# Attention pipeline: where the routing units, the table operations and the experts' first transposes stand in the order of work

## The chip, the cores and the metric

The kernel runs on one core of a Trainium2 chip. The metric is the device time of one execution in microseconds (us). The engines are TensorE (PE for its matrix products, PEld for its weight loads), VectorE (DVE), ScalarE (ACT), GpSimd (POOL) and SyncE (SP, which issues transfers). Each takes its own instructions strictly in the order in which they are written and waits for the others by semaphores.

## The reference

Sliding window attention with sinks, then a mixture of experts over its output, all in float32:

```python
B, H, S, D = 4, 8, 768, 64;  n_sink, window = 4, 128
scores = scale * np.matmul(q, k.transpose(0, 1, 3, 2))
scores = np.where(is_sink | in_window, scores, -1e9)
a = np.exp(scores - scores.max(-1, keepdims=True))
a = a / (a.sum(-1, keepdims=True) + 1e-09)
x = np.matmul(a, v).transpose(0, 2, 1, 3).reshape(3072, 512)      # the tokens

g_idx = np.argmax(x @ w_group, axis=1)              # 4 groups
e_idx = np.argmax(x @ w_expert[g], axis=1)          # 4 experts in each, within the token's group
out[token] = softmax(group)[g_idx] * softmax(expert)[e_idx] * (np.maximum(x @ w1[g, e], 0) @ w2[g, e])   # F = 1024
```

## The kernel before, in words

**Attention.** The 3072 tokens are 24 tiles of 128 rows (`NI`), six to a sequence (`NT`). A loop `for i in range(NI + 2)` runs as a pipeline over them: step i makes the scores of tile i, transposes the weights of tile i-1 and multiplies them with the values, and finishes tile i-2 ("old", `b`). The heads come in two groups of four. On VectorE one step is: a predicated copy that puts the sinks in (`ps<-selu,ps`), four masked maxima (`sm<-ps,msk`), the same again for the second group, in even steps the reduction and reciprocal of the sums (`rc`), the normalised logits (`lw`), the row normalisation `norm(b)` (`xt<-po,rc`, which writes the finished rows), and what stands behind it. ScalarE makes the exponentials (`pt`), copies the transposed weights (`pw`, once for each group) and the values (`xT`). GpSimd masks the copied weights with a triangle (`pw<-pw,tri`, once for each group). TensorE's products of step i+1 with the values (`po<-pw,vv`) come behind the `xt` of step i, since both use `po`; `xt` itself comes behind the sinks' product (`po<-spT,sv`).

**Routing.** A generator, `route_batch`, does the routing of six tiles at a time, in small VectorE instructions ("units"), and yields between them. There are four batches; three of them ("early") run within the attention loop, the fourth in its tail. A yield tells of what kind the next piece is: `None` is a plain unit, "pe" stands ahead of products on TensorE, "rd" ahead of a VectorE instruction that reads them, and "hv" ahead of a table operation. The loop takes pieces at fixed places by `routing(k, kinds)`, which takes up to k pieces if the next one is of a kind that is wanted. `unit(k)` takes one plain unit; a step has a quota of eight (`REND`). Units stand between the maxima of the second group (two places), ahead of `norm` (four) and at the end of the step (two); "rd" and "hv" pieces stand only behind `norm`. The names in the profile: `rev`, `m` (shown as `ps`), `rdt`, `req`, `og`, `oh` open a batch (one-hots of group and expert), `pe`, `rs`, `runb`, `pos`, `ge`, `ga` count the position of each token in its expert, `row`, `rm`, `rss` make its gate; a table operation is `bf` on VectorE (one-hot of the position) with `af` on GpSimd, two halves to a batch; the product `tp<-af,bf` is then added to `tab`. From the table come the indices of an expert's tokens (`sel`, `gidx`, `idz`, `sidx`), and from the counts the choice of the next expert (`cnt`, `ktmp`, `cs`, `key`, `ktop`, `keid`, `eid`).

A part of the small tiles of batches 0 and 1 (`keep`) lives in PSUM, in the bank of the second group's scores (`psb[1]`, shown as `ps`); those of batch 2 live in SBUF.

**Weights.** Each expert weight is split in two parts, `whi` on ScalarE and `wlo<-rw,whi` on VectorE. From step 18 on a step may hold such a split of 128x512; its VectorE half (`late()`) stands behind `norm`.

**The tail and the experts.** After the last tile the loop runs two more steps (i = 24, 25) in which the experts begin: `early_work` transposes the first expert's two token tiles (`ph<-ident,xg`; `xpose`, which also casts them on ScalarE and takes the rest on VectorE, both named `un`), then starts its first layer (`ph<-un,whi`). After the loop the experts run one after the other.

All instructions carry line 105, that of the helper that issues them, so groups are told apart by names.

Of the kernel before, what the change touches and what calls it, by code (L numbers as in the profile page):

```python
# [24 lines left out]
NT = S // P  # L25
NI = B * NT
# [29 lines left out]
XLEAD = 9  # L56
PEGAP = 1.6
REND, TSTEP = 8, 16
UNITS = {}
HC = 3  # L60
LATE = 6
PELAG = 2.0
# [72 lines left out]
def moe_attention(tc, kqT, vN, vS, nsw, wgx, w1, w2, out):  # L135
    nc = Pinned(tc)
    v = nc.vector
    with ExitStack() as top, ExitStack() as att:
# [38 lines left out]
        psb = [ps_s.tile([P, 4, 256], F32, name=f"ps{g}") for g in range(2)]  # L177
        PART = 3 * BW + NSK + MAXB
# [174 lines left out]
        def put_gates(n):  # L353
            for _ in range(min(n, len(gates))):
                t, g = gates.pop(0)
                nc.sync.dma_start(xd[t * P:(t + 1) * P, DM:XW], g)
# [7 lines left out]
        def route_batch(i0, nb, lt, wk, pt, tab, na, pick=None):  # L364
# [3 lines left out]
            early = pt is None and not tail  # L368
# [7 lines left out]
            keep = early and pick in (None, 0)  # L376
# [18 lines left out]
            o5 = sm([nk, 4], "req")  # L395
# [4 lines left out]
            yield  # L400
            v.tensor_reduce(m, o5a, AX.X, ALU.max)
            yield
            og = psb[1][:, :, PART - nb:PART].rearrange("p c n -> p n c") if keep else o5[:, :, 0]
            if keep:
                o5b, mb = (t.rearrange("p a (b k) c -> p a b k c", k=nk) for t in (o5a, wide(m)))
                v.tensor_tensor(og.rearrange("p (a b) c -> p a b c", a=na2), o5b[:, :, :, 0], mb[:, :, :, 0], ALU.is_equal)
            v.tensor_tensor(o5a, o5a, wide(m), ALU.is_equal)
# [1 line left out]
            oh = wk.tile([P, nb, NE], BF16, name=f"oh{nb}", bufs=1)  # L409
            v.tensor_tensor(oh.rearrange("p n (g e) -> p n g e", g=G), o5[:, :, 1:],  # L410
                            og[:, :, :, None].to_broadcast([P, nb, G, EG]), ALU.mult)
            yield "pe"
            pp = misc(pt)
            pc = pp[:, nb * NE:(nb + 1) * NE]
# [277 lines left out]
        regs, raws, wt, half, held = {}, [], {}, [], {}  # L692
# [213 lines left out]
        rb = []  # L906
# [308 lines left out]
        def early_work(q):  # L1215
            plan.update(todo=[], at=0, next=0)
            for j in range(q["nt"]):
                xpose(q, j, True)
                yield 0.43
            for k, us in enumerate(layer1_wide(q)):  # L1220
                if k == LATE:
                    wait_for("late")
                    xpose(PARTS[0][1], 0, True)
                yield us

        quota = [0]

        def unit(k):
            if quota[0] > 0 and routing(1, (None,)):
                quota[0] -= 1  # L1230

        ew = early_work(PARTS[0][0])
        load_s(0)
        for i in range(NI + 2):
            live = i < NI
            quota[0] = UNITS.get(i, REND)
            a, b = i - 1, i - 2
            mid, old = 0 <= a < NI, 0 <= b < NI
            state["clk"] += 3.0
            if i == NI:  # L1240
                flush()
                state.update(gap=0.0, dve=state["clk"])
                sps.close()
                put_gates(MAXB)
                while later:
                    gather(*later.pop(0))
                ps_h = fl.enter_context(tc.tile_pool(name="ps_h", bufs=4, space=PSUM, side="right", reuse_waits="tile"))
                tail.append(ps_h)
            if live:
                scores(i, 0)  # L1250
            if mid:
                evac(a, 0)
            if i == NI and half:
                half.pop()()()
            if old:
                if b < NI - 1:
                    values(b, 1)
                out_evac(b)
            if live:
                load_v(i)  # L1260
                scores(i, 1)
                issue()
                maxima(i, 0)
                warm(FILL[i] if i < len(FILL) else 0, tp2[:, 0, 256:448])
            if mid:
                sink_copy(a)
                halves(a, 0)
            if i == NI + 1:
                state["at"] = 0.0
                routing(1, ("pe",))  # L1270
            if mid:
                if not live:
                    next(ew)
                    next(ew)
                sink_t(a)
                trans(a, 1)
            if live:
                exps(i, 0, (0, 1))
            if mid:
                evac(a, 1)  # L1280
                sink_evac(a)
            if live:
                exps(i, 0, (2, 3))
            if mid and not live:
                halves(a, 1)
            if not live and later and not gates:
                gather(*later.pop(0))
            late = None
            if live:
                late = half.pop()() if half else wjob()  # L1290
                if half and i % NT == 0:
                    first, more = late, half.pop()
                    late = lambda: (first(), more()())
            if i == 0:
                late_consts()
            if i == 1:
                routing_consts()
            if live:
                maxima(i, 1, lambda k: unit(k) if k else None)
            if old:  # L1300
                natural(b)
            state["clk"] += 3.0
            if old:
                logits(b)
            if live and mid:
                values(a, 0)
            if i % 2 == 0 and 0 < i <= NI:
                sums(i - 1)
            if not live:
                norm(b)  # L1310
                norm_logits(b)
                next(ew)
            if mid and not live:
                values(a, 0)
            add_heads()
            routing(1, ("pe",))
            if mid:
                sink_values(a)
            if live and old:
                norm_logits(b)  # L1320
            if live:
                if mid:
                    halves(a, 1)
                flush()
                exps(i, 1)
                trans(i, 0)
                for k in range(4):
                    unit(k)
                if old:
                    norm(b)  # L1330
                if later and not gates:
                    gather(*later.pop(0))
                put_gates(2)
                if late:
                    late()
                routing(1, ("rd",))
                routing(1, ("hv",))
                for k in range(2):
                    unit(k)
            else:  # L1340
                if mid:
                    values(a, 1)
                    next(ew)
                put_gates(MAXB)
                routing(TSTEP, (None, "rd", "hv"))
            if old:
                del env[b]
            if i >= CHOOK:
                prefetch(min(RAW, len(raws) + (1 if live else RAW)))
            if not live:  # L1350
                wjob()
                next(ew, None)
# [295 lines left out]
```

## Time and profile before

| what | value |
|---|---|
| median of 3 runs | 487.56 us (487.55 to 487.65) |
| the profiled execution | 487.55 us, its span 485.7 us, 1.85 us around it |
| granted clock of TensorE, mean | 0.998 |
| busy, share of the span | PE 95%, DVE 70%, ACT 67%, POOL 34% |
| attention with routing | up to about 150 us of the span, then the experts |

A busy share over the whole span mixes two stages: the attention loop, in which four engines hand work to each other within a step of some 5 to 7 us, and the experts, in which TensorE alone has hardly a gap. In the timeline's rows a bracket behind a row is the idle time of that engine ahead of it, and what ended it.

### The profile page before, as it was taken

To read this page: it belongs to the slowest core of one execution; us is meant where nothing else is said; L and a number is where in the kernel's file an instruction comes from. 1 tells how busy PE (TensorE), PEld (TensorE's weight loads), DVE (VectorE), ACT (ScalarE), POOL (GpSimd) and SP (SyncE) were. 2 spreads that over 40 slices of the span, in tenths; PEclk is the share of its full clock that TensorE was granted. 3 is DMA by queue.
4 is the path that set the end of the run, shared out by engine and by line. 5 is a ranking of instruction groups with operands and counts; after the bars stand their busy time and mean duration, and the time that the engine had idled before them with its cause. 6 is when DMAs were issued, how large, how long until landed. Compare 5 with 4: busy or idle time off the path is not lost.

```text
span 485.7 us, 15514 instructions
## 1 busy us (share of the span) xinstructions
PE 462.8 (95%) x5865; PEld 394.7 (81%) x5865; DVE 341.5 (70%) x1143; ACT 325.9 (67%) x875; POOL 163.8 (34%) x269
## 2 busy tenths in 40 slices
PE   7999999998879999999999999999999999999994
PEld 6887778776768987989888778797979788877894
DVE  6766787888897799893075256563788888788870
ACT  4898889889884353772265275655778787687961
POOL 3463675565656022323203033012402160205021
PEclk9999999999999999999999999999999999999999
DMA  6566567577764469795124388858969997968200
GB/s 192 162 200 206 192 181 215 181 232 259 263 203 137 132 202 360 242 360 217 47 70 148 109 282 289 306 218 305 381 216 373 410 384 249 301 210 298 63 26 31
DMA packets 49556, 107.47 MB, mean 221 GB/s; under 512 B 8932, under 2 KB 9444, under 8 KB 49472
## 3 DMA queue, kind: packets, MB, share of 16 engines
q1 hardware_dynamic: 45008, 93.17, 56.7%
q0 software_dynamic: 4320, 12.94, 7.7%
q8 instruction: 48, 0.79, 0.7%
q10 hardware_dynamic: 144, 0.28, 0.2%
q14 instruction: 36, 0.29, 0.2%
HBM read 93.58 MB, written 12.93 MB: 219 GB/s over the span
## 4 chain that ended last, share of the span: by engine, by line
PE 65%; DVE 13%; issue 8%; ACT 6%; DMA 4%; POOL 2%; SPq 1%; POOLq 0%; DVEq 0%; ACTq 0%
PE po L105 29%; PE ph L105 28%; PE tp L105 4%; PE ps L105 4%; DVE wlo L105 3%; ACT pt L105 2%; DVE sm L105 2%; DVE xt L105 2%; ACT whi L105 1%; DMA rw<-in_w 1%; DVE un L105 1%; DMA vv<-in_vN 1%; DVE ps L105 1%; DMA ni<-in_nsw 1%; SPq L105 1%
## 5 line engine op out<-in xcount | busy, mean ns | idle before, releaser
L105 DVE TENSOR_TENSOR wlo<-rw,whi 128x1024 fp32r<-128x1024 f32 (+1 forms) x116 | 134.9, 1187 | 28.3 <-ACT whi L105 27.9
L105 PE MATMUL ph<-un,whi 128*128 128x256 f32 (+9 forms) x576 | 128.8, 313 | 0.1
L105 PE MATMUL po<-whi,un 128*128 128x512 f32 (+6 forms) x384 | 126.3, 394 | 0.0
L105 ACT CAST whi<-rw 128x1024 fp32r<-128x1024 f32 (+1 forms) x116 | 114.8, 1018 | 5.7 <-PE po L105 3.5
L105 POOL DMA_INDIRECT out<-ot,sidx x33 | 41.7, 1264 | 221.0 <-ACT ot L105 164.3
L105 PE MATMUL ph<-un,wlo 128*128 128x160 f32 (+10 forms) x416 | 99.6, 265 | 0.2 <-DVE wlo L105 0.2
L105 PEld LDWEIGHTS ph<-un,whi 128*128 128x128 f32 x576 | 94.0, 189 | 2.4 <-issue 0.6
L105 PEld LDWEIGHTS po<-whi,un 128*128 128x128 f32 (+5 forms) x384 | 69.8, 183 | 19.3 <-issue 2.1
L105 ACT ACTIVATE pt<-sm,st 128x136 f32<-128x136 f32 x192 | 76.2, 404 | 7.9 <-DVE st L105 7.7
L105 PE MATMUL po<-wlo,un 128*128 128x512 f32 (+7 forms) x200 | 77.9, 389 | 0.0
L105 PEld LDWEIGHTS ph<-un,wlo 128*128 128x128 f32 x416 | 76.8, 190 | 0.8 <-DVE wlo L105 0.4
L105 POOL TENSOR_TENSOR pw<-pw,tri 128x512 f32<-128x512 f32 x40 | 51.6, 1289 | 17.9 <-ACT pw L105 17.0
L105 DVE CUSTOM_DVE_ANT_0 sm<-ps,msk 128x136 f32<-128x136 f32 x192 | 46.3, 296 | 7.2 <-ACT xT L105 1.4
L105 PE MATMUL po<-pw,vv 64*64 64x128 f32 (+1 forms) x1408 | 40.9, 250 | 7.0 <-POOL sp L105 2.3
L105 PEld LDWEIGHTS po<-pw,vv 64*64 64x64 f32 x1408 | 34.9, 133 | 13.4 <-POOL sp L105 8.2
L105 POOL DMA_INDIRECT xg<-xd,gidx x33 | 35.1, 1065 | 29.4 <-DMA rw<-in_w 16.1
L105 PE MATMUL ps<-kb,qb 64*64 64x204 f32 (+1 forms) x768 | 41.9, 331 | 3.1 <-DVE bf L105 2.1
L105 PEld LDWEIGHTS po<-wlo,un 128*128 128x128 f32 (+6 forms) x200 | 35.7, 179 | 7.8
L105 DVE TENSOR_TENSOR hc<-ph,hc 128x160 f32<-128x160 f32 (+6 forms) x64 | 21.5, 337 | 26.2 <-ACT hc L105 26.2
L105 ACT ACTIVATE un<-ph 128x256 fp32r<-128x256 f32 (+1 forms) x40 | 15.3, 383 | 36.4 <-PE ph L105 36.0
L105 ACT ACTIVATION_READ_ACCUMULATOR pt<-sm,st 128x1 f32 x192 | 37.2, 194 | 0.0
L105 ACT ACTIVATE ot<-po,cg 128x512 f32<-128x512 f32 (+7 forms) x25 | 17.0, 679 | 29.3 <-PE po L105 29.2
(226 smaller groups left out, 654.6 us busy)
## 6 DMA issues: line engine op xcount, KB each, us to landing
rw<-in_w SPq DMA_DIRECT2D x128, 512.0 KB, 5.9
kb<-in_kqT SPq DMA_DIRECT2D x23, 272.0 KB, 4.6
qb<-in_kqT SPq DMA_DIRECT2D x24, 256.0 KB, 3.7
vv<-in_vN SPq DMA_DIRECT2D x24, 256.0 KB, 3.7
xd<-xt SPq DMA_DIRECT2D x24, 256.0 KB, 2.7
xg<-xd,gidx POOLq DMA_INDIRECT x33, 5.8
out<-ot,sidx POOLq DMA_INDIRECT x33, 5.9
sv<-in_vS SPq DMA_DIRECT2D x4, 128.0 KB, 3.7
```

The costliest lines, as they stand in the source:

```text
L105: r = f(*a, **k)
```

## The change

1. Ahead of `norm`, `fill(n)` takes the place of up to four `unit`s: n is 2 in even steps (those with the sums), 4 in odd steps, and 0 where the tile that is normalised is the first of a sequence (i = 2, 8, 14, 20). `fill` takes plain units and table operations ("hv"), and a table operation counts as two.
2. Behind `norm` the order was `late()`, "rd", "hv", two units. It is now "rd", `fill` of two (five where there was none ahead of `norm`; one less in a step with a weight split), and then `late()`.
3. `og` of batch 2 goes to PSUM too while `oh` is made, with one small instruction more; later uses read it in SBUF as before.
4. In step 24 the transposes of the first expert's two token tiles stand ahead of the split and of the products with the values, no longer behind them.

```diff
-UNITS = {}
+HOLE = 2, 4
@@ route_batch
-            og = psb[1][:, :, PART - nb:PART].rearrange("p c n -> p n c") if keep else o5[:, :, 0]
-            if keep:
+            og = psb[1][:, :, PART - nb:PART].rearrange("p c n -> p n c") if early else o5[:, :, 0]
+            if early:
...
             oh = wk.tile([P, nb, NE], BF16, name=f"oh{nb}", bufs=1)
             v.tensor_tensor(oh.rearrange("p n (g e) -> p n g e", g=G), o5[:, :, 1:],
                             og[:, :, :, None].to_broadcast([P, nb, G, EG]), ALU.mult)
+            og = og if keep else o5[:, :, 0]
             yield "pe"
@@ the loop
+        def fill(n):
+            while n > 0 and quota[0] > 0:
+                big = bool(rb) and rb[0][2] == "hv"
+                if not routing(1, (None, "hv")):
+                    return
+                n -= 1 + big
+                quota[0] -= 1 + big
...
-            quota[0] = UNITS.get(i, REND)
+            quota[0] = REND
...
-            if i == NI and half:
-                half.pop()()()
+            if i == NI:
+                next(ew)
+                next(ew)
+                if half:
+                    half.pop()()()
             if old:
                 if b < NI - 1:
                     values(b, 1)
...
             if mid:
-                if not live:
-                    next(ew)
-                    next(ew)
                 sink_t(a)
                 trans(a, 1)
...
-                for k in range(4):
-                    unit(k)
+                fill(HOLE[i % 2] if i % NT != 2 else 0)
                 if old:
                     norm(b)
                 if later and not gates:
                     gather(*later.pop(0))
                 put_gates(2)
+                routing(1, ("rd",))
+                fill((2 if i % NT != 2 else 5) - (late is not None))
                 if late:
                     late()
-                routing(1, ("rd",))
-                routing(1, ("hv",))
-                for k in range(2):
-                    unit(k)
```

VectorE around the row normalisations of steps 18, 19 and 20, the maxima left out. Before:

```order
L105 TENSOR_TENSOR xt<-po,rc 128x2x4x64
L105 TENSOR_TENSOR wlo<-rw,whi 128x512 x2
L105 TENSOR_TENSOR bf<-colm,ps_99 128x384
L105 COPY_PREDICATED ps_98<-selu,ps_98 128x4x64
...
L105 TENSOR_TENSOR xt<-po,rc 128x2x4x64
L105 TENSOR_TENSOR wlo<-rw,whi 128x512
L105 TENSOR_TENSOR bf<-colm,ps_99 128x384
L105 COPY_PREDICATED ps_98<-selu,ps_98 128x4x64
...
L105 TENSOR_TENSOR xt<-po,rc 128x2x4x64
L105 TENSOR_TENSOR wlo<-rw,whi 128x512
L105 TENSOR_TENSOR tab<-tab,tp 128x112
```

The same place with the change, up to the split of step 19:

```order
L105 TENSOR_TENSOR bf<-colm,ps_99 128x384
L105 TENSOR_TENSOR xt<-po,rc 128x2x4x64
L105 TENSOR_TENSOR bf<-colm,ps_99 128x384
L105 TENSOR_TENSOR wlo<-rw,whi 128x512 x2
L105 COPY_PREDICATED ps_98<-selu,ps_98 128x4x64
...
L105 TENSOR_TENSOR xt<-po,rc 128x2x4x64
L105 TENSOR_TENSOR tab<-tab,tp 128x112
L105 TENSOR_TENSOR sel<-tab,oh_202 128x32
L105 TENSOR_REDUCE ps_99<-sel 128x2
L105 TENSOR_TENSOR wlo<-rw,whi 128x512
```

Both table operations of batch 1 stand around the `xt` of step 18, ahead of the splits, and the table is added to one step earlier; on TensorE its product `tp<-af,bf` comes in step 19 in place of step 20. In step 20 five instructions that open batch 2 then stand between `xt` and the split.

VectorE from the `xt` of step 22 to the maxima of step 23, before (`ISA sm` is a masked maximum, most of them left out):

```order
L105 TENSOR_TENSOR xt<-po,rc 128x2x4x64
L105 TENSOR_TENSOR wlo<-rw,whi 128x512
L105 TENSOR_TENSOR pe<-tp,oh_3190 128x96
L105 COPY cnt<-tp 128x16
L105 TENSOR_TENSOR ktmp<-oh_202,cnt 128x16
L105 TENSOR_REDUCE cs_203<-ktmp 128x1
L105 SCALAR_TENSOR_TENSOR key<-cnt,col 128x16
L105 SCALAR_TENSOR_TENSOR key<-oh_202,key 128x16
L105 COPY_PREDICATED ps_98<-selu,ps_98 128x4x64
...
L105 TENSOR_REDUCE ktop<-key 128x1
```

The same work with the change, from the `xt` of step 21 to the maxima of step 22:

```order
L105 TENSOR_TENSOR xt<-po,rc 128x2x4x64
L105 TENSOR_TENSOR pe<-tp,oh_3131 128x96
L105 COPY cnt<-tp 128x16
L105 TENSOR_TENSOR ktmp<-oh_202,cnt 128x16
L105 TENSOR_REDUCE cs_203<-ktmp 128x1
L105 TENSOR_TENSOR wlo<-rw,whi 128x512
...
L105 SCALAR_TENSOR_TENSOR key<-cnt,col 128x16
L105 SCALAR_TENSOR_TENSOR key<-oh_202,key 128x16
L105 ISA sm,st<-ps_99,msk 128x136
...
L105 TENSOR_REDUCE ktop<-key 128x1
```

The counts, the key and the expert's choice all come one step earlier; the split has moved behind the counts, and the two `key` instructions now stand between maxima of the second group, where `ktop` stood; `ktop` stands behind the last of them.

ScalarE in step 24, from the copy of the weights to the one that follows. Before:

```order
L105 COPY pw<-tp 128x2x4x64
L105 CAST whi<-rw 128x512
L105 COPY xT<-po 128x2x2x128
L105 CAST un<-ph 128x4x128 x2
L105 COPY pw<-tp 128x2x4x64
```

With the change:

```order
L105 COPY pw<-tp 128x2x4x64
L105 CAST un<-ph 128x4x128 x2
L105 CAST whi<-rw 128x512
L105 COPY xT<-po 128x2x2x128
L105 COPY pw<-tp 128x2x4x64
```

The two casts of the first expert's tokens have moved ahead of the split and of `xT`; on TensorE the eight transposes have moved ahead of the first sixteen products with the values.

## Rows read from the trace of the kernel before

**Rows 1.** The page, parts 1 and 4 (the chain that ended last).

```profile
PE 462.8 (95%) x5865; PEld 394.7 (81%) x5865; DVE 341.5 (70%) x1143; ACT 325.9 (67%) x875; POOL 163.8 (34%) x269
...
PE 65%; DVE 13%; issue 8%; ACT 6%; DMA 4%; POOL 2%; SPq 1%; POOLq 0%; DVEq 0%; ACTq 0%
```

**Rows 2.** Windows: stretch, length, busy us (instructions), clock, DMA share, GB/s.

```profile
42.00:67.00 25.00, 23.42 (x603) 19.39 (x600) 19.54 (x104) 21.00 (x86) 12.25 (x24) 1.00 0.59 194
206.00:300.00 94.00, 94.00 (x621) 79.20 (x620) 46.34 (x87) 46.30 (x84) 21.54 (x22) 1.00 0.54 182
```

**Rows 3.** Chain of waits, 140 to 152 us: start us, us, what.

```profile
143.34 0.74 DVE ktmp L105
...
146.60 1.01 DVE ge L105
...
148.88 0.61 DVE un L105
...
149.53 1.58 PE ph L105 x11
```

**Rows 4.** Timeline of step 11: start us, us, engine, operation, idle before.

```profile
71.40 0.69 DVE L105 TENSOR_TENSOR xt<-po,rc 128x512 f32<-128x512 f32 x1 [1.03 <-ACT pt L105]
...
72.00 0.55 DVE L105 TENSOR_TENSOR bf<-colm,ps 128x384 fp32r<-128x384 f32 x1
```

**Rows 5.** Timeline of step 14 around its row normalisation.

```profile
87.08 0.15 DVE L105 COPY ps<-rev 128x4 f32<-128x4 f32 x1
...
88.49 0.68 DVE L105 TENSOR_TENSOR xt<-po,rc 128x512 f32<-128x512 f32 x1
```

**Rows 6.** Timeline of step 16 around its row normalisation.

```profile
100.26 0.33 DVE L105 TENSOR_REDUCE ps<-oh 128x16 f32<-128x96 bf16 x1
...
100.73 0.69 DVE L105 TENSOR_TENSOR xt<-po,rc 128x512 f32<-128x512 f32 x1
...
101.57 0.34 PE L105 MATMUL po<-pw,vv 64*64 64x128 f32 x4 [0.80 <-DVE xt L105]
```

**Rows 7.** Timeline of step 18's end and the start of step 19.

```profile
113.93 0.55 DVE L105 TENSOR_TENSOR bf<-colm,ps 128x384 fp32r<-128x384 f32 x1
...
114.54 0.57 PE L105 MATMUL ps<-kb,qb 64*64 64x204 f32 x8 [1.61 <-DVE bf L105]
```

**Rows 8.** Timeline of step 20's end.

```profile
122.80 0.88 PE L105 MATMUL tp<-af,bf 128*128 128x112 f32 x6
...
124.43 0.69 DVE L105 TENSOR_TENSOR xt<-po,rc 128x512 f32<-128x512 f32 x1 [1.03 <-PE po L105]
...
125.03 0.73 DVE L105 TENSOR_TENSOR wlo<-rw,whi 128x512 fp32r<-128x512 f32 x1
...
125.68 0.26 DVE L105 TENSOR_TENSOR tab<-tab,tp 128x112 f32<-128x112 f32 x1
...
126.03 0.58 ACT L105 COPY pw<-tp 128x512 f32<-128x512 f32 x1 [1.09 <-DVE tab L105]
...
126.69 1.28 POOL L105 TENSOR_TENSOR pw<-pw,tri 128x512 f32<-128x512 f32 x1 [1.48 <-ACT pw L105]
...
126.78 0.42 DVE L105 COPY_PREDICATED ps<-selu,ps 128x256 f32<-128x256 int32 x1
```

**Rows 9.** Timeline of step 21's end.

```profile
132.58 1.41 POOL L105 TENSOR_TENSOR pw<-pw,tri 128x512 f32<-128x512 f32 x1 [0.28 <-ACT pw L105]
...
132.77 1.33 DVE L105 TENSOR_TENSOR oh<-req 128x96 bf16<-128x96 f32 x1
```

**Rows 10.** Tile view of `oh`: durations in ns (min/median/max), first and last start.

```profile
L105 DVE TENSOR_TENSOR oh<-req,ps x2: 253/254/255, 55.2 to 89.6; 128x96 bf16<-128x96 f32 x2
```

**Rows 11.** Timeline of step 23, between the second group's maxima.

```profile
142.74 0.16 DVE L105 TENSOR_REDUCE ktop<-key 128x1 f32<-128x16 f32 x1
...
142.76 1.28 POOL L105 TENSOR_TENSOR pw<-pw,tri 128x512 f32<-128x512 f32 x1
...
143.25 0.82 DVE L105 SCALAR_TENSOR_TENSOR ktmp<-key,ktop,col 128x16 f32<-128x16 f32 x1
```

**Rows 12.** Tile view of `ktmp`, the same instruction with its input in PSUM.

```profile
L105 DVE SCALAR_TENSOR_TENSOR ktmp<-ps,ktop,col x1: 231/231/231, 98.0 to 98.0; 128x16 f32<-128x16 f32 x1
```

**Rows 13.** Timeline of step 24.

```profile
145.92 0.90 PE L105 MATMUL po<-pw,vv 64*64 64x128 f32 x32 [1.67 <-POOL sp L105]
...
146.75 1.09 PE L105 MATMUL ph<-ident,xg 128*128 128x128 f32 x8
...
147.44 1.07 ACT L105 CAST un<-ph 128x512 fp32r<-128x512 f32 x2
```

## The prediction

> **What bounds the kernel now.** I read the page first. TensorE is busy 95% of the span and stands for 65% of the chain that ended last; VectorE has 13% of it [rows 1]. The windows say where the two belong: in the experts TensorE is busy for 94.00 of 94.00 us, in a stretch of attention for 23.42 of 25.00, with VectorE, ScalarE and GpSimd at 19.54, 21.00 and 12.25 [rows 2]. So the experts have no hole, and whatever the attention wins or loses reaches the end only by moving the start of the first expert's layer. The chain of waits shows what released that start, at 149.53 us: VectorE's last `un`, and ahead of it, on VectorE, `ktmp` with 0.74 and `ge` with 1.01 us [rows 3]. At the end of attention VectorE's list is the path. In earlier steps it is a ring: `xt` waits for TensorE's sinks' product or has a hole (1.03 us in step 11 [rows 4], 1.03 in step 20 [rows 8]), the next products with the values wait for `xt` (0.80 in step 16 [rows 6]), and the next predicated copy waits for all that VectorE has behind `xt`.
>
> A unit taken from ahead of `xt` therefore releases TensorE sooner, and one put behind `xt` delays the maxima, and with them ScalarE's exponentials, by the same amount. No unit is left out, so the change pays only where a unit comes into a hole or leaves the neighbourhood of something that makes it wait.
>
> The second thing that the trace shows is such a neighbourhood. `oh` of batch 2, with its inputs in SBUF, took 1.33 us and ended just as GpSimd's triangle mask (132.58, 1.41 us) did [rows 9]; with `og` in PSUM the same instruction took 0.25 twice [rows 10]: 1.08 us of waiting. `ktmp` with `key` in SBUF took 0.82 and ended with GpSimd's mask [rows 11], with its input in PSUM 0.23 [rows 12]: 0.59 of waiting. `ge`, the third, took 1.01 [rows 3]. The Trainium skill, "GPSIMD Engine Reference", § 8 Key points, has this as a rule: GpSimd shares its SBUF interfaces with VectorE, and VectorE's instructions with two SBUF inputs contend with it. The trace agrees by the three pairs just named, and the rule speaks against part 2 of the change, whose splits (both inputs in SBUF) come later in the step, nearer to the mask.
>
> **The change part by part.** Shifts are of VectorE's work against the profiled execution (487.55 us, span 485.7 and 1.85 around it, at the median of 487.56); minus is earlier.
>
> *Steps 8 to 13, batch 0.* Both `bf` (0.55 each) come ahead of step 11's `xt`, into its hole of 1.03 [rows 4], where they cost about 0.1 and free as much behind two later `xt`. But the product of the table, 0.88 as in step 20 [rows 8], comes a step earlier on TensorE, ahead of the sinks' product that `xt` waits for. I take 0; bounds -0.6 (both `bf` are won, less their half that the maxima must wait for anyway) and +0.5 (0.88 less what is left of the hole).
>
> *Steps 14 to 17, batch 1.* Step 14 opens with five instructions ahead of `xt` that end at 88.49, 1.41 us after 87.08 [rows 5]; all now stand behind it. `xt` comes up to 1.4 sooner, the copy behind it as much later: nearly nothing. Step 16 has three pieces ahead of `xt` and no longer the last two, from 100.26 to 100.73 [rows 6]: 0.47 that TensorE waits less, of its 0.80. Two others (`pos`, `ge`) are pushed out from behind `xt` into the next step's maxima, which pass them between instructions. I take -0.55; bounds 0 (they return in step 18, where there is no hole left) and -1.0 (step 14 keeps half of its 1.41 as well).
>
> *Steps 18 to 20, the table of batch 1.* Behind step 18 the `bf` at 113.93 holds up TensorE's scores of the second group, 1.61 us of idle time [rows 7]; with `bf` ahead of the splits that wait goes and the copy comes 0.55 sooner. In step 19 the product of 0.88 comes ahead of `xt`, which loses that again and 0.3 more, and `tab`, `sel` and its sum take the place of `bf` (six instructions in the 1.10 us from 125.68 to 126.78 [rows 8], so some 0.55 for three: no difference). In step 20 the hole of 1.03 shrinks by 0.88, of which the index instructions, now between the maxima, take half (0.55), and the five opening instructions (1.41 [rows 5]) replace six that took 1.10: +0.3. Together -0.55 + 0.88 - 0.33 + 0.3 = +0.3; bounds -0.2 (the 0.88 is fully covered by ScalarE's exponentials, and half of the 1.03 is won) and +0.9 (no hole is won back in step 20).
>
> *Step 20's split.* It stood right behind `xt`, at 125.03, long before the mask at 126.69, which was late because ScalarE's copy of the weights waited 1.09 us for `tab` [rows 8]. `tab` is gone from there, so that copy starts at about 124.9, the mask 0.66 later (126.03 to 126.69), at 125.6; and the split comes at 125.03 - 0.45 + 1.41 = 126.0. It stands in the mask's 1.28 us. The waits bound it: 0 if the mask is later by half a microsecond (as in step 14's order, where ScalarE is late), 1.1 by `oh` [rows 9, 10]. I take the middle, +0.5. Behind the split are the copy and all of step 21's maxima.
>
> *Step 21.* `oh` loses its 1.08, and stands between maxima; of this 0.55 is won behind `xt`, since the counts (`pe` to `cs`, some 0.5) now stand there, and 0.4 is paid ahead of `xt`, where TensorE has batch 2's position products a step earlier and VectorE one instruction more for `og`. -0.15; bounds -0.55 and +0.2.
>
> *Steps 22 and 23, the key.* `ktmp` leaves the mask's time: -0.59. It comes ahead of step 22's `xt` with two others, in the place of the two `key` instructions behind it: +0.24. That is -0.35. But both `key` stand where `ktop` stood, and `ktop` began at 142.74, the mask at 142.76 [rows 11]: the first goes before it or waits, the second mostly falls into it. No wait: 0; a whole mask of 1.28 less 0.2: 1.1. I take `ktmp`'s 0.59, as the nearest row, since it is the same tile at the same mask: +0.6.
>
> *The tail.* In step 24 TensorE idles 1.67 us ahead of its products with the values [rows 13], and the transposes of 1.09 fit in there. `ge` leaves the mask, 0.8 won. Against this `runb`, in SBUF now, may wait out half of step 23's mask, and four more units stand ahead of its `xt`. And ScalarE's order puts the two casts (1.07) ahead of `xT`, which the fourth batch's logits on TensorE wait for ahead of the first layer: most of the 1.09 is given back. I take -0.3; bounds 0 and -1.0.
>
> The sum is 0 - 0.55 + 0.3 + 0.5 - 0.15 - 0.35 + 0.6 - 0.3 = +0.05: 487.6 us, no difference that counts. A measurement of this kernel can tell about 0.2%, which is 1.0 us: 486.6 to 488.5.
>
> **The rivals.**
>
> *Faster: the collisions miss.* If neither step 20's split nor the `key` waits for a mask, the two terms of +1.1 go: 487.55 - 1.05 = 486.5. For it: three waits of 1.08, 0.59 and 0.8 stand on the path before, and the change takes all three away from their masks; the new ones depend on tenths of a microsecond. Batch 1 at its bound of -1.0 and the table at -0.2 carry it to 485.6. Against: the `key` stands within 0.02 us of where a mask started.
>
> *Slower: the split and the `key` both wait a mask out.* The place is the end of step 20, the price 1.1 and 1.1 in place of 0.5 and 0.6: 487.55 + 1.15 = 488.7, with the table's upper bound 489.3. It decides from the point where the mask of step 20 starts ahead of 126.0. For it is that `tab`'s wait, which kept the mask late, is what the change itself removes. Taken alone, the skill's rule would have every moved split wait behind a mask; by that the result would be this one.
>
> *Nothing arrives.* The attention is shorter by more than 1 us, but the first layer then waits for ScalarE's casts or the split weights in step 24: 487.3 to 487.6. The 65% that TensorE has of the chain [rows 1] is for it; that the chain's last link ahead of the experts is VectorE [rows 3] is against it.
>
> **How the numbers follow.** The sum as it stands, with one of the waits or two halves, has a chance of 0.34, its own range 486.6 to 488.5; that nothing arrives 0.06; the two waits missed 0.37; both waited out 0.23. The first two are "within 0.2%", so faster 0.37, same 0.40, slower 0.23. The range takes in most of both other cases: 485.7, the faster rival with batch 1 and the table near their bounds, to 489.1, the slower with half of the table's upper bound.
>
> **What would show it.** Right: no 1.61 us of idle time behind a `bf` in front of step 19's scores; `oh` at about 0.25 in all batches and `ktmp` at 0.2; the ends of attention agree within 1 us at the first layer's first product (149.5). Step by step: step 20's split and the two `key` at their own lengths (0.7, 0.2) or up to 1.1 longer. Wrong would make it above all a mask whose start moves with ScalarE, and a VectorE that is not the path in the tail, so that neither the waits nor their absence reach 149.5.

## The result, and the profile after

The changed kernel took 490.41 us (median of 8 executions, 487.59 to 492.04), the kernel before, measured beside it on the same chip, 487.66 (8 executions, 487.03 to 488.37). The ratio is 1.0052, with an interval of 1.0029 to 1.0075: slower by half a per cent. It lies above the range of the forecast. The execution that was profiled took 492.04 us, with a span of 490.3, so it shows the loss at its largest; its mean granted clock was 0.989, where the kernel before had 0.998. The sizes of the steps below are those of single profiled executions, the verdicts those of all. The first product of the first expert's layer came at 152.53 us in place of 149.07, so 3.5 of the 4.6 us by which the span grew lie in the attention; most of the rest lies in a stretch right behind it in which TensorE's clock was low.

Part 1 of the page after, to compare with [rows 1]:

```profile
PE 466.3 (95%) x5865; PEld 397.4 (81%) x5865; DVE 343.9 (70%) x1144; ACT 325.8 (66%) x875; POOL 165.7 (34%) x269
```

One VectorE instruction more and 2.4 us more of its busy time; 3.5 us more on TensorE, which has not one instruction more. So instructions have become longer. Windows of TensorE alone say where its 3.5 us come from (columns: stretch, length, busy us and instructions, granted clock, DMA share, GB/s):

```profile
112.00:117.00 5.00, 3.55 (x102) 1.00 0.75 248
117.00:122.00 5.00, 5.00 (x81) 0.66 0.63 208
...
150.00:156.00 6.00, 5.08 (x74) 0.72 0.84 234
```

Two stretches run below the upper level of 2.4 GHz. Microsecond by microsecond, the clock stands at 0.50, the lower level of 1.2 GHz, from shortly before 118 to 121 and from 152 to 155 us; the kernel before has 1.00 in every microsecond of its attention. Ahead of each fall TensorE had idled: 3.55 us of the five ahead of the first were busy. That alone doesn't make the clock fall: in the same five microseconds the kernel before was busy for 3.39, and its clock stayed up.

What made it idle is, in the main, VectorE. Timeline of the end of step 18 (start us, us, engine, operation, idle before), to compare with [rows 7]:

```profile
112.32 1.99 POOL L105 TENSOR_TENSOR af<-oh,av 128x336 fp32r<-128x336 bf16 x2
...
112.67 2.19 DVE L105 TENSOR_TENSOR wlo<-rw,whi 128x512 fp32r<-128x512 f32 x2
...
114.26 0.67 POOL L105 COPY sp<-pt 128x32 f32<-128x32 f32 x1
...
114.98 0.27 PE L105 MATMUL tp<-ident,sp 64*128 64x64 f32 x2 [0.96 <-POOL sp L105]
```

The 1.61 us of idle time behind `bf` are gone, as foretold, but both of GpSimd's table halves now run back to back beside the two splits, the two engines hold each other up (1.99 and 2.19 us), and the small copy `sp` behind them makes TensorE wait 0.96 us. Then step 20, to compare with [rows 8]:

```profile
127.47 1.27 POOL L105 TENSOR_TENSOR pw<-pw,tri 128x512 f32<-128x512 f32 x1 [0.28 <-ACT pw L105]
...
127.62 1.67 DVE L105 TENSOR_TENSOR wlo<-rw,whi 128x512 fp32r<-128x512 f32 x1
...
129.22 0.42 DVE L105 COPY_PREDICATED ps<-selu,ps 128x256 f32<-128x256 int32 x1
...
130.69 0.67 PE L105 MATMUL ps<-wsd,xT 128*64 128x40 f32 x16 [1.29 <-DVE st L105]
...
132.53 0.25 DVE L105 TENSOR_TENSOR oh<-req,ps 128x96 bf16<-128x96 f32 x1
...
132.84 0.22 PE L105 MATMUL tp<-oh,trib 128*128 128x96 bf16 x1 [0.66 <-ACT whi L105]
...
133.33 0.72 PE L105 MATMUL po<-spT,sv 64*128 64x128 f32 x8
...
134.15 0.69 DVE L105 TENSOR_TENSOR xt<-po,rc 128x512 f32<-128x512 f32 x1 [1.13 <-ACT pt L105]
```

The split begins 0.15 us behind the start of the mask and ends 0.55 behind its end: 1.67 us in place of 0.73. The maxima, ScalarE and TensorE (1.29 us idle) wait for it. `oh` takes 0.25, so its old wait [rows 9] is gone; but `oh` now stands behind the late maxima. TensorE's position products, which read it, start 0.06 us behind its end (their row names ScalarE's `whi`, which ended at about the same moment), and they stand ahead of the sinks' product (`po<-spT,sv`) that step 21's `xt` needs. And step 22, to compare with [rows 11]:

```profile
138.25 1.29 POOL L105 TENSOR_TENSOR pw<-pw,tri 128x512 f32<-128x512 f32 x1
...
138.37 1.20 DVE L105 SCALAR_TENSOR_TENSOR key<-cnt,col 128x16 f32<-128x16 f32 x1
...
141.19 0.92 PE L105 MATMUL ps<-kb,qb 64*64 64x204 f32 x16 [1.31 <-DVE lw L105]
...
141.76 1.27 POOL L105 TENSOR_TENSOR pw<-pw,tri 128x512 f32<-128x512 f32 x1 [0.28 <-ACT pw L105]
...
142.24 0.83 DVE L105 TENSOR_SCALAR oh<-key,ktop 128x16 f32<-128x16 f32 x1
```

The first `key` begins 0.12 us behind the start of a mask and takes 1.20 us, until the mask has ended; the one-hot of the expert falls into the next, 0.83 us against 0.23 in PSUM or outside a mask.

The steps, from one `xt` to the next, worked out from their starts in the timelines (the last column is an experiment below, `e16_fills`, the same order with TensorE's holes filled, whose clock stayed up):

| step | before | changed | filled |
|---|---|---|---|
| 2 to 17 | 85.54 | 85.92 | 85.81 |
| 18 | 5.04 | 5.09 | 5.09 |
| 19 | 6.82 | 8.21 | 7.37 |
| 20 | 6.42 | 5.81 | 5.81 |
| 21 | 7.09 | 8.53 | 8.76 |
| 22 | 6.71 | 7.48 | 7.48 |
| 23 | 6.85 | 6.51 | 6.63 |
| 24 | 4.93 | 4.21 | 4.22 |
| 25 | 7.97 | 9.95 | 8.45 |

### The profile page after: what moved, and what is told of

It reads as the page before. It is cut to its first block, busy times and chain, and to the rows that moved or that the text cites. A ratio compares the mean times of both kernels' runs of the same rounds, so it can differ in the third digit from the quotient of the medians.

```text
span 490.3 us, 15514 instructions
## 1 busy us (share of the span) xinstructions
PE 466.3 (95%) x5865; PEld 397.4 (81%) x5865; DVE 343.9 (70%) x1144; ACT 325.8 (66%) x875; POOL 165.7 (34%) x269
## 4 chain that ended last, share of the span: by engine, by line
PE 69%; DVE 11%; ACT 8%; issue 8%; POOL 1%; DMA 1%; POOLq 0%; DVEq 0%; ACTq 0%
PE po L105 30%; PE ph L105 28%; PE ps L105 6%; PE tp L105 5%; ACT pt L105 4%; DVE wlo L105 3%; ACT whi L105 2%; DVE sm L105 1%; ACT pw L105 1%; DMA ni<-in_nsw 1%; DVE xt L105 1%; DVE ps L105 1%; POOL out L105 1%; DVE un L105 1%; ACT xT L105 1%
## 5 line engine op out<-in xcount | busy, mean ns | idle before, releaser
L105 DVE TENSOR_TENSOR wlo<-rw,whi 128x1024 fp32r<-128x1024 f32 (+1 forms) x116 | 136.3, 1199 | 28.5 <-ACT whi L105 28.0
```

Of the source, the lines that this page charges most:

```text
L105: r = f(*a, **k)
```

## The experiments

Theory A, formed on this: the new order puts VectorE's instructions with two inputs in SBUF beside GpSimd's work, three to four waits follow, TensorE idles behind them, and is then granted the lower clock. Theory B: the experts' transposes cost. Theory C, a rival from `e5_late` on: the order costs by itself, since what stood ahead of something now stands behind it. Each kernel was timed beside the kernel before, whose median was between 487.19 and 487.64 us. Times of different experiments are better compared by their ratios; with their intervals, differences of under 1 us or so between two of them are not told from none.

**The order alone** (`e1_order`).

From the changed kernel, with the two `next(ew)` of step 24 back ahead of `sink_t(a)` as well:

```diff
-            og = psb[1][:, :, PART - nb:PART].rearrange("p c n -> p n c") if early else o5[:, :, 0]
-            if early:
+            og = psb[1][:, :, PART - nb:PART].rearrange("p c n -> p n c") if keep else o5[:, :, 0]
+            if keep:
...
-            og = og if keep else o5[:, :, 0]
```

> The new order of units, table operations and splits alone; og of batch 2 stays in SBUF and the experts' transposes stay where they were. Theory A (the new order puts VectorE's instructions with two SBUF inputs into GpSimd's masks and table operations, and the idle TensorE behind these waits is then granted the lower clock): nearly all of the loss is here, 489 to 491 us, with splits or key instructions of over 1 us and one or two stretches at a granted clock of 0.50. Theory B (the transposes, or the casts that ScalarE makes of them ahead of xT, are what costs): about 487.6.

489.69 us, ratio 1.0046 (1.0029 to 1.0062). The splits of step 18 took 2.19, that of step 20 1.67, the key 1.20, the one-hot 0.83 us, as in the changed kernel. The loss is in the order. Its profiled execution had no stretch at the lower clock and still took 53.98 us from the `xt` of step 17 to that of step 25, where the kernel before took 51.83, so the waits cost by themselves. (Its span was 488.3, with a part of the excess in the experts.)

**`og` alone** (`e2_og`).

From the kernel before:

```diff
-            og = psb[1][:, :, PART - nb:PART].rearrange("p c n -> p n c") if keep else o5[:, :, 0]
-            if keep:
+            og = psb[1][:, :, PART - nb:PART].rearrange("p c n -> p n c") if early else o5[:, :, 0]
+            if early:
...
+            og = og if keep else o5[:, :, 0]
```

> The kernel before with og of batch 2 in PSUM and nothing else. Theory A: oh takes 0.25 in place of 1.33 us, its wait goes, and the time falls by up to 1.0 us, to 486.6 to 487.2. Theory B says nothing of it. Rival to A: the wait only moves to the next instruction, 487.6.

486.77 us, ratio 0.9989 (0.9973 to 1.0004): half a microsecond or so, not told from none by this interval. The wait itself is gone, in the timeline:

```profile
132.51 0.24 DVE L105 TENSOR_TENSOR oh<-req,ps 128x96 bf16<-128x96 f32 x1
```

**The experts' transposes alone** (`e3_ew`).

From the kernel before:

```diff
-            if i == NI and half:
-                half.pop()()()
+            if i == NI:
+                next(ew)
+                next(ew)
+                if half:
+                    half.pop()()()
...
-                if not live:
-                    next(ew)
-                    next(ew)
                 sink_t(a)
```

> The kernel before with the transposes of the first expert's tokens ahead and nothing else. Theory A: TensorE's 1.67 us of idle time in step 24 takes them in, and the first layer starts up to 0.5 us sooner: 487.0 to 487.6. Theory B: the casts hold up xT by 1.0 us, the first layer starts later and TensorE idles long enough ahead of it to be granted the lower clock: 488.5 to 490.

487.77 us, ratio 1.0007 (0.9994 to 1.0020): neither the gain nor the loss. Theory B falls. Its profiled execution, the slowest at 490.23 us, shows something else. In step 21, where its order is that of the kernel before, `oh` happened to wait longer (1.82 us in place of 1.33), TensorE idled 1.33 in place of 0.85 behind it, and the clock stood at 0.50 from 138 to beyond 141 us. So the lower clock is not the changed kernel's alone.

**Two holes filled** (`e4_fill`).

From the changed kernel:

```diff
+                if i == 19:
+                    warm(8, tp2[:, 0, 64:256])
                 sink_t(a)
...
+            if i == NI:
+                warm(8, tp2[:, 0, 64:256])
             if old:
                 natural(b)
```

> The changed kernel with eight small products of zeros (128x192, bf16, result never read) in each of two of TensorE's holes: ahead of step 19's sink transposes and ahead of step 24's row transposes. Nothing else differs. Theory A: the granted clock stays at 1.00 through attention and the first layer, and of the loss the 2.9 us that the two stretches at 0.50 cost go: 487.3 to 488.5. Rival (the clock falls for another reason than these two holes): 490 or more, with the two stretches still there.

490.83 us, ratio 1.0070 (1.0046 to 1.0094): no gain. The first stretch at 0.50 was gone, but another came behind the hole of step 21 (130 to 136.5 us), which had not been filled; and the second filling made its own hole longer, since it wrote to a bank that ScalarE had still to read:

```profile
151.75 0.82 PE L105 MATMUL tp<-wz 128*128 128x192 bf16 x8 [1.58 <-ACT spT L105]
```

Taken as a whole, this one decides nothing.

**The split back in its place** (`e5_late`).

From the changed kernel:

```diff
+                if late:
+                    late()
                 routing(1, ("rd",))
                 fill((2 if i % NT != 2 else 5) - (late is not None))
-                if late:
-                    late()
```

> The changed kernel with the weight split back ahead of the pieces behind the row normalisation; the rest of the change stays. Theory A (waits behind GpSimd's mask): the split of step 20 takes 0.7 in place of 1.67 us, and those of step 18 no longer lie beside both of GpSimd's table operations: 1.0 to 1.5 us sooner than the changed kernel, 488.5 to 489.5. Rival C (the order of the units itself costs, since what stands ahead of the split now stands behind it): no gain, 490 or more.

487.19 us, ratio 1.0004 (0.9990 to 1.0018), 1.3 us under the lower end of what the theory had. Step 20's split took 0.68 us. By a few tenths the key missed its mask too (0.17), so more than one wait went at once. Its profiled execution still has a stretch at 0.50, from 114 to 122 us.

**Counts and key in PSUM** (`e6_key`).

From the changed kernel:

```diff
-                n_e = psb[1][:, 3, PART:PART + NE] if keep else cnt
+                n_e = psb[1][:, 3, PART:PART + NE] if keep or early and pick == 1 else cnt
...
-                yield from pick_id(wk, pick, n_e, keep)
+                yield from pick_id(wk, pick, n_e, keep or early and pick == 1)
```

> The changed kernel with batch 2's counts and key in PSUM, as those of batch 0 are; the order of the instructions is the same. Theory A: key takes 0.2 in place of 1.20 us and the one-hot of the expert 0.23 in place of 0.83; the time falls by 1.0 to 1.6 us, to 489 or so. Rival C: the order costs, not the wait; less than 0.5 us.

487.87 us, ratio 1.0014 (0.9996 to 1.0032). The order is the changed kernel's to the last instruction, only two small tiles lie elsewhere, and 2.5 us go (0.4 to 3.3 by the two intervals), so C doesn't explain the loss. Both `key` instructions took 0.18, the second of them begun within a mask, and the one-hot 0.22 us; the splits were still 2.19 and 1.67. Its profiled execution shows the waits gone but not what they were worth, since its clock stood at 0.50 from 130 to beyond 136 us. In the next two kernels, with the same tiles in PSUM and the clock up there, steps 22 and 23 took 12.8 us together, where the filled one of the table took 14.1 (in these the split is back too).

**Both** (`e7_late_key`).

> Both at once: the split back in its place and batch 2's counts and key in PSUM. Theory A: the two add up, 2.0 to 3.0 us off the changed kernel, and with the waits go stretches at the lower clock: 487 to 488, as the kernel before or a little under it. Rival C: 489 or more.

488.49 us, ratio 1.0019 (0.9999 to 1.0038), in executions from 486.01 to 490.71: no better than either alone, a miss. Its executions fall into two kinds by their mean granted clock: three at 0.997 and 0.998 took 486.01 to 486.49 us, nine at 0.993 and less 487.86 to 490.71. In the profile, which is one of the latter, the windows of TensorE are:

```profile
112.00:117.00 5.00, 2.96 (x66) 0.88 0.75 229
117.00:122.00 5.00, 5.00 (x54) 0.50 0.31 110
```

and the hole ahead of it, in the timeline, is one that the split back in its place brings again, with the second `bf` behind both splits:

```profile
114.26 0.75 PE L105 MATMUL ps<-kb,qb 64*64 64x204 f32 x12 [2.04 <-DVE bf L105]
```

**That hole filled** (`e13_fill`).

From the kernel with both:

```diff
                 load_v(i)
+                if i == 19:
+                    for _ in range(20):
+                        nc.tensor.matmul(tp2[:, 0, 256:384], wz[:, 0:P], wz[:, 0:P], start=True, stop=True)
                 scores(i, 1)
```

> The kernel with the split back and the key in PSUM, and twenty products of zeros (128x128, bf16, result never read) in TensorE's hole of 2.04 us ahead of step 19's second scores; VectorE's order is the same. Theory A with the clock: the stretch at 0.50 that followed this hole goes, the granted clock is 0.995 or more and the time 486.0 to 487.0. Rival: the clock still falls there, 488 to 489.

486.55 us, ratio 0.9981 (0.9969 to 0.9993), ten of eleven executions at a clock of 0.996 or more. VectorE's order is that of the kernel with both, and 1.9 us go with the stretch at 0.50: this is the run that shows the clock's part. Step 19 took 8.11 us, where the kernel with both took 9.99. The profiled execution, 488.09 us, is the eleventh: it had a stretch at 0.50 elsewhere, from 148 to beyond 151 us. The same windows:

```profile
112.00:117.00 5.00, 4.10 (x92) 1.00 0.80 234
117.00:122.00 5.00, 4.33 (x90) 1.00 0.52 153
```

**The tables apart** (`e8_table`).

From the changed kernel:

```diff
-                fill((2 if i % NT != 2 else 5) - (late is not None))
+                fill((2 if i % NT != 2 else 5) - (late is not None), (None,))
```

The second argument of `fill` names the kinds that it takes; it is new.

> The changed kernel with table operations only ahead of the row normalisation: the two of batch 1 then stand in steps 18 and 19, not both around step 18's xt, and GpSimd's two halves are a step apart. Theory A (its three waits: the splits beside both table halves in step 18, step 20's split, the key): the splits of step 18 take 1.4 to 1.6 together in place of 2.19 us and TensorE's 0.96 us hole there goes, so that the first stretch at the lower clock mostly goes; 1 to 2 us sooner than the changed kernel, 488.5 to 489.5. Rival C (only the waits behind the masks count): no gain.

486.33 us, ratio 0.9982 (0.9970 to 0.9995), every execution at a clock of 0.995 or more: 4 us off the changed kernel, 2 more than expected, and a little faster than the kernel before. The splits of step 18 took

```profile
110.85 0.70 DVE L105 TENSOR_TENSOR wlo<-rw,whi 128x512 fp32r<-128x512 f32 x1
...
112.38 0.84 DVE L105 TENSOR_TENSOR wlo<-rw,whi 128x512 fp32r<-128x512 f32 x1 [0.83 <-ACT whi L105]
```

with one table half beside them. It also puts the table's product back into step 20, where the split reached only the latter part of a mask (1.13 us), and the counts and the key of batch 2 back behind the `xt` of step 22. The key still waited (1.19). So this is not a test of the tables alone: from step 18 to 25 it is 2.3 us shorter than the filled kernel of the table, and 0.65 of that lie in steps 19 and 20.

**All three** (`e10_apart`: split back, key in PSUM, tables apart).

> Split back in its place, key in PSUM and the table operations apart: no hole of TensorE of over 1.0 us should be left between 105 and 150 us. Theory A with the clock (the lower clock follows TensorE's holes): the granted clock is 0.995 or more in nearly all executions, and the time that of the executions of the former kernel at such a clock, 486.0 to 486.7. Rival (the lower clock comes by itself in some executions of whatever kernel): its executions scatter from 486 to 490.5 again.

484.88 us, ratio 0.9949 (0.9933 to 0.9964), 1.1 us under the expectation, all six executions between 484.23 and 485.81 at a clock of 0.997 or more. It beats both kernels. What is left of a hole is in step 21, where the opening of batch 2 stands ahead of the scores:

```profile
125.34 0.92 PE L105 MATMUL ps<-kb,qb 64*64 64x204 f32 x16 [1.30 <-DVE ps L105]
```

**The same without the transposes ahead** (`e14_apart_ew`).

> The fastest version so far (split back, key in PSUM, tables apart) with the experts' transposes back behind the products with the values. If the transposes ahead gain what the forecast gave them: 0.3 us slower than it, 485.2. If the casts ahead of xT cost more than they gain: 0.3 to 0.8 us faster, 484.1 to 484.6.

484.97 us, ratio 0.9957 (0.9942 to 0.9972): no difference. The fourth part of the change is worth nothing here either way.

**The kernel before with its tiles in PSUM** (`e9_og_key`: `og`, counts and key of batch 2, nothing moved).

> The kernel before, in its own order, with batch 2's og, counts and key in PSUM. Theory A: besides the wait of oh (1.08 us) that of ktmp (0.59) goes, 1.0 to 1.7 us sooner than before: 485.6 to 486.3. Rival: waits there are hidden by ScalarE, and the time stays within 0.5 us of the kernel before.

486.14 us, ratio 0.9975 (0.9965 to 0.9986): 1.1 us for three small tiles. `ktmp`, 0.82 in [rows 11], in its timeline:

```profile
141.76 0.23 DVE L105 SCALAR_TENSOR_TENSOR ktmp<-ps,ktop,col 128x16 f32<-128x16 f32 x1
```

**The early steps' order alone** (`e11_early`: the change up to step 17, and the tiles in PSUM).

From the changed kernel with the key in PSUM, the transposes back; behind `norm` come `late()`, "rd", and from step 18 on "hv" and two units as before:

```diff
-                fill(HOLE[i % 2] if i % NT != 2 else 0)
+                if i < 18:
+                    fill(HOLE[i % 2] if i % NT != 2 else 0)
+                else:
+                    for k in range(4):
+                        unit(k)
```

> The change's order in steps up to 17 alone (batches 0 and 1, no splits there), the order before from step 18 on, the experts' transposes where they were, and batch 2's og, counts and key in PSUM. Theory A (the early batches gain what the forecast gave them, the loss is all behind step 18): 0.3 to 0.7 us under the kernel before with the same tiles in PSUM, 485.4 to 485.9. Rival: the early order gains nothing, 486.1.

486.36 us, ratio 0.9976 (0.9963 to 0.9988), no better than the former: a miss. What the steps up to 17 gain does not reach the end, or is not there in most executions.

**Four holes filled** (`e15_fills`: as `e4_fill`, and ten products ahead of step 21's logits, fourteen of 128x128 ahead of step 23's scores; step 24's into a bank that nobody reads).

> The changed kernel, VectorE's and ScalarE's order untouched, with products of zeros (result never read) in TensorE's four holes: ahead of step 19's sink transposes, ahead of step 21's logits, ahead of step 23's scores, and in step 24 ahead of the row transposes, this time into a bank that nobody reads. Theory A with the clock: the granted clock is 0.995 or more, and what is left over the kernel before is the waits alone, 1.0 to 2.0 us: 488.2 to 489.3. Rival (the clock is no part of the loss, or falls all the same): 490 or more.

492.29 us, ratio 1.0092 (1.0073 to 1.0111): the worst. Step 21's filling itself waited for ScalarE's copies from its bank, made a hole of 2.18 us of one of 1.29, and the clock fell behind it:

```profile
130.67 0.98 PE L105 MATMUL tp<-wz 128*128 128x192 bf16 x10 [2.18 <-ACT spT L105]
```

**Four holes filled, once more** (`e16_fills`: step 21's filling, of eight, ahead of its sink transposes; step 24's of six).

> As the filling of four holes, with the one of step 21 ahead of its sink transposes, where no copy of that bank is under way; VectorE's and ScalarE's order is that of the changed kernel. Theory A with the clock: no stretch at 0.50 in most executions, and the time is the kernel before plus the waits alone, 488.0 to 489.3. Rival (the clock is no part of the loss): 490 or more.

489.70 us, ratio 1.0034 (1.0021 to 1.0046), 488.23 to 490.60, six of seven executions at 0.997 or more, and the seventh at 0.995. Its windows beside the two low stretches of the changed kernel:

```profile
117.00:122.00 5.00, 4.92 (x106) 1.00 0.64 215
...
150.00:156.00 6.00, 5.66 (x115) 1.00 0.83 226
```

With the clock up the order alone, with what the fillings themselves cost, is 2.1 us slower than the kernel before (1.0 to 2.2 by the interval). That is 0.4 above the upper end of what the theory gave the waits. What fillings would cost in the kernel before was not measured.

## Why the prediction was wrong

It said 487.6 us and no difference; the kernel is slower. The slower rival, "the split and the `key` both wait a mask out", had the mechanism, was priced at 488.7 and given 0.23. By the filled column of the table, where the clock stayed up, the terms compare so: steps 18 to 20 forecast at +0.3, measured at 0.0; step 20's split and step 21 together +0.35, measured +1.67; steps 22 and 23 +0.25, measured +0.55; steps 24 and 25, the tail's, -0.3, measured -0.2. So the largest part of the loss lies in one place, between the `xt` of step 20 and that of step 21.

**Steps 8 to 17** (0 and -0.55). Not shown as a gain. From step 2 to 17 the changed kernel took 0.38 us longer than the one before, other kernels with the same order between 0.3 longer and 1.3 shorter. The mean of all thirteen is 84.95 us, that of the four with the old order there 85.42: a gain of the foretold size is possible, but single executions scatter by more, and the early order alone gave nothing that could be measured.

**Steps 18 to 20, the table** (+0.3). The place was right (`bf` no longer holds TensorE up, the product of 0.88 comes ahead of step 19's `xt`), but the step left out GpSimd's side: the two `af` halves, a step apart before, became one piece of 1.99 us beside two splits that took 2.19, and the copy behind them kept TensorE waiting. With the clock up, step 19 took 7.37 against 6.82 and step 20 gave back 0.6, so the sum of the term was not what failed. Tables apart, the kernel lost all its excess, but that moved the counts and the key too.

**Step 20's split** ("I take the middle, +0.5"). This is the first step that failed. The working put the split at 126.0 and the mask at 125.6 to 126.9, so it stood in the mask by its own numbers; the middle between nothing and 1.1 was not supported by them. It waited 0.9 to 1.0, nearly the upper bound of 1.1.

**Step 21** (-0.15). `oh` lost its 1.08, as foretold. But step 21 took 1.44 longer (1.67 with the clock up). With the split back in its place it took 7.54 (`e5_late`), so the split explains 1.0 to 1.2, and some 0.45 is a cost where the term had a gain: the position products, put ahead of the sinks' product, stand behind `oh` and the maxima. That these products are the reason is read from the timeline and not tested by a run of its own.

**Steps 22 and 23, the key** (-0.35 + 0.6). `ktmp` at 0.23 was right. The key waited 1.0, not the 0.59 of the nearest row, since it stands earlier in the mask than `ktmp` did; "mostly falls into it" stood in the text, and half was taken all the same. That the expert's one-hot would then stand in the next step's mask (0.6 lost) was not seen.

**The tail** (-0.3). Steps 23 and 24 gained 0.9 with the clock up, step 25 gave back 0.5. The first layer's transposes ahead are worth nothing.

**What no step had: the clock.** The waits of VectorE open holes of 0.9 to 2 us on TensorE, and behind some of them TensorE ran at 0.50 for 3 to 7 us. In the changed kernel every execution had a mean clock of 0.993 or less; of the kernel before, only 4 of the 118 executions beside the experiments had 0.994 or less (487.99 to 489.17 us). What it costs is seen best among executions of one kernel: with the split back 486.22 to 487.06 us at 0.996 or more and 487.31 to 489.31 at 0.994 or less; with both, and in `e4_fill`, the medians of the two kinds lie 2.1 and 3.0 us apart. With the order alone there is no such division (488.41 and 490.08 us at 0.997 and 0.998, 487.78 to 491.03 below). The difference of the medians of the changed kernel and the one with its holes filled, 490.41 to 489.70, is 0.7 us, less what the fillings themselves cost; with the split back and the key in PSUM, where one hole was followed by the lower clock, it was 1.9 us. So of the 2.75 us lost some 2.1 are the order's waits and the rest the clock, if the medians are taken as they stand; their intervals, 1.4 to 3.7 and 1.0 to 2.2 us over the kernel before, leave that division open. A change that forecasts more idle time on TensorE may have such a cost on top. Why some holes are followed by the lower clock and others not these runs don't settle. Their length alone doesn't decide it: in the profiled execution of the changed kernel the clock fell behind holes of 0.96 and 0.92 us and not behind those of 1.29 and 1.31, while the kernel before has two of 1.61 and 1.67 and none of its microseconds was lower.

## What to carry to other kernels

Two queues that share something are planned together: before an instruction is moved, write down what the other engine runs at its new place, and where the two overlap by your own numbers, price the whole wait, not its middle. Which of two begins first matters: a split took its own 0.7 us when it began ahead of a mask, and 1.67 when it began 0.15 us behind the mask's start. Where an order of instructions is good and only one operand makes it wait, move the operand (three tiles of 16 to 24 columns in PSUM were worth 1.1 us), not the instruction. A wait that leaves the densest engine idle is priced again when that engine's clock may fall behind it; look at the granted clock of the stretch before taking a sum of durations as the time.

## What the runs showed of the hardware

VectorE's instructions with two SBUF inputs and GpSimd's work took turns in these traces: what began while the other engine's instruction ran got on only when that one had ended. `key`, `ktmp` and the one-hot ended 0.03 us behind the end of the mask that they began in. Splits ended 0.55 us behind the end of the mask or table half that they began in, whatever their start: 0.91 us long in the kernel before, 1.00, 1.13 and 1.67 in the changed one. A split that began ahead of the mask kept its own length (0.69), and a table half that began beside it took 1.25 us where it takes 0.78 otherwise. The Trainium skill, "GPSIMD Engine Reference", § 8 Key points, says that the two contend when VectorE's instruction has two SBUF inputs; the runs agree. They add that with one operand in PSUM an instruction begun within a mask does not wait: the second `key` 0.18 us (`e6_key`), the one-hot 0.23 (`e7_late_key`), `ktmp` 0.23 (`e9_og_key`).

The effects of single edits did not add up: by their ratios the split back gave 2.3 us over the changed kernel and the key in PSUM 1.9, but both together 1.6. Each of them also changed which holes TensorE had, and with them the clock of the executions. All three edits together gave 5.0.

A filling of zeros whose destination lay in a bank from which ScalarE had still to copy waited itself: the holes became 1.58 and 2.18 us long, where they had been 0.92 and 1.29.
